# Hash-masked attention and a gated feed-forward block: a hand-written instruction order, transposes on TensorE for the first six pairs, a hash over both heads at once and two-bank accumulators

## The chip, the cores and the metric

The kernel runs on one core of one Trainium2 chip. The core has TensorE (matmuls, PE in the profile), VectorE (DVE), ScalarE (ACT), GpSimd (POOL) and SyncE (SP, which here only starts DMAs). TensorE writes into PSUM, of which the kernel allots eight banks of 512 fp32 numbers per partition. The metric is the device time of one execution in microseconds (us).

## The reference

Inputs are q, k and v of shape (4 batches, 8 heads, 768 tokens, 64), a projection proj (64 x 6), and four weight matrices. Attention is restricted to queries and keys that fall into the same hash bucket; its output is the token matrix x (3072 x 512) of a gated feed-forward block with a gated residual.

```python
q_bits = (np.einsum('bhsd,dk->bhsk', q, proj) > 0).astype(np.int64)
k_bits = (np.einsum('bhsd,dk->bhsk', k, proj) > 0).astype(np.int64)
q_bucket = np.sum(q_bits * 2 ** np.arange(6), axis=-1)   # k_bucket likewise
mask = q_bucket[:, :, :, None] == k_bucket[:, :, None, :]
scores = np.where(mask, scale * np.matmul(q, k.transpose(0, 1, 3, 2)), -1e9)
attn = softmax(scores)                    # with + 1e-09 under the sum
x = (attn @ v).transpose(0, 2, 1, 3).reshape(3072, 512)
...
ffn_out = (gelu(x @ w_gate) * (x @ w_val)) @ w_out
return x + sigmoid(x @ w_res) * ffn_out
```

## The kernel before

Two heads form a pair; there are 16 pairs, four per batch of 768 tokens. The mask needs no comparison: six hash bits of each token, as +0.5 or -0.5, and a constant row are appended to the 64 channels of q and k, scaled so that one differing bit pushes the score far below. So scores of a head contract 71 rows (64 + 6 + 1). A constant 2^-90 times the sum of v keeps a row without any match finite (`L228`).

**Preparation of a pair** (`prep`). q, k and v are loaded by DMA from SP's queue (`load`, L120 and L125). POOL casts q and k to bf16 into the padded tiles `nat` (128 columns per head and token block, L138 and L140). VectorE transposes 32 x 32 blocks of the raw values (`t32`, L168), TensorE multiplies them with `projw` (hash, L175: one matmul per head, half of the channels, and side, 192 columns, four sides next to each other in four column groups of the array). VectorE transposes the sums back (L181) and writes the bits into `nat` with 16 small operations per group of two pairs (L186). Then one DMA transpose per side turns `nat` (12 blocks of 128 x 128, over half padding) into `aug` with channels on partitions (L191). POOL casts v and sums it (L145 to L153).

**Attention** (`scores`, `values`). A head's 768 x 768 score block is cut into banks of 512 columns; a chunk is two banks, nine chunks make a pair. Per chunk: score matmuls into `sp` (L255), one exponential on ScalarE over 1,024 columns (L260), and eight matmuls with the exponentials as weights into the accumulator `av` (L235), which are issued one chunk later. `av` is one bank per head in two rotating buffers. `finish` divides by the sum (L214, L215) into `x_tok` and starts a DMA transpose of the pair's x into `x_sb` (L218).

**Feed-forward** (`gate_val`, `project`). Per batch, `gate_val` runs 12 x 16 matmuls (L276) with a Gelu on ScalarE (L282) and a product on VectorE (L283). `project` is the output side: per token tile, four matmuls of the residual gate (`rps`, L293), a Tanh (L296), twelve matmuls (`fps`, L300) and two VectorE operations (L305, L307), then the store. It is a generator of five pieces per tile; 24 of its 30 pieces are spread over the next batch's chunks, one per chunk, and the last ones (`HELD`) run in the first chunks of the batch after it. `gate_val` of batch b-1 starts in the fourth chunk of batch b (`LEAD = 4`). `rps` and `fps`, the hash sums and the warm-up share the pool `mm_ps`, two rotating buffers of one bank.

**Order.** The Python loop emits the work, and the tile framework's scheduler then orders each engine's instructions by its own estimates. So hash matmuls and single `rps` or `fps` matmuls stand between chunks where the source doesn't put them. DMAs of SP's queue start in that queue's order; a waiting DMA holds those behind it. Fourteen matmuls on zeros (L314) run at the start.

The softmax here doesn't subtract the row's maximum and nothing guards it: scores larger than these inputs give would overflow.

## Time and profile before

| what | us |
|---|---|
| median of 2 runs | 407.17 (406.35 to 407.98) |
| the profiled execution | 406.82 |
| its span, first to last instruction | 404.7 |
| TensorE busy (matmuls) | 366.9, mean granted clock 0.92 |
| ScalarE busy | 206.9 |
| VectorE busy | 170.7 |
| POOL busy | 81.5 |

Groups of instructions that the steps of the prediction use:

```profile
L260 ACT ACTIVATE e<-sp 128x1024 bf16<-128x1024 f32 x144 | 144.4, 1022 | 83.8 <-PE sp L255 82.4
L168 DVE STREAM_TRANSPOSE t<-ld 128x384 f32<-128x384 f32 x64 | 33.8, 557 | 43.8 <-DMA ld<-in_q_dram 21.3
L175 PE MATMUL hs<-t,projw 128*32 128x192 f32 x256 | 27.3, 375 | 17.8 <-DVE t L168 11.7
L186 DVE TENSOR_SCALAR nat<-ht 32x72 bf16<-32x72 f32 x128 | 31.3, 244 | 2.3
```

A line names the source line, the engine, the operation, output<-input with shapes and the count; then busy us in all and mean ns of one; then the idle time of the engine just before these, and what ended it. The page's other parts are the busy share in 40 equal slices, the chain of work that ended last, and the DMA queues: loads of q, k and v land 4.6 to 5.0 us after issue (median), the 32 DMA transposes of q and k 4.9, the 16 of x 3.7, the stores 2.1. HBM traffic is 29.37 MB read and 6.29 MB written.

### The profile page before, as it was taken

The numbers are of one execution on the slowest core, as the hardware profiler recorded it, in microseconds if no ns is written. First come the engines' busy times: TensorE is split into PE (matmuls) and PEld (weight loads), VectorE is DVE, ScalarE is ACT, GpSimd is POOL, SyncE is SP. The second block draws the span as 40 slices with busy tenths as digits, with TensorE's granted clock in tenths as the row PEclk, the third lists the DMA queues.
The fourth block names the chain that finished last, engine by engine and source line by source line (L and its number), as shares of the span: only waits on it lengthen the run. The fifth ranks groups of instructions, "written<-read, shape, count | busy, mean of one in ns | idle before, by whom it ended". The sixth has DMA issues, their size and how long they took to land. (4 is left out here: it accounts for less than half of the span.)

```text
span 404.7 us, 7265 instructions
## 1 busy us (share of the span) xinstructions
PE 366.9 (91%) x2944; PEld 202.2 (50%) x2990; DVE 170.7 (42%) x366; ACT 206.9 (51%) x225; POOL 81.5 (20%) x149
## 2 busy tenths in 40 slices
PE   6386969959999999998999999899999999999995
PEld 2133524425566555554665555556655555565542
DVE  3727123715433324734336537443336232333342
ACT  2036534636332877773335886863357788333210
POOL 7456245344300022241000342310000000000000
PEclk9759555865999999999999999999999999999999
DMA  7999999996910048776000973920008221100012
GB/s 220 223 270 245 159 239 285 201 238 142 238 55 2 28 84 188 137 186 202 2 0 2 185 205 85 185 47 2 0 2 158 76 68 47 45 2 0 16 65 78
DMA packets 86177, 46.61 MB, mean 115 GB/s; under 512 B 64640, under 2 KB 83072, under 8 KB 86144
## 3 DMA queue, kind: packets, MB, share of 16 engines
q1 hardware_dynamic: 79488, 40.91, 44.7%
q0 software_dynamic: 6336, 5.24, 8.7%
q8 instruction: 23, 0.38, 0.4%
q14 instruction: 10, 0.08, 0.1%
q10 hardware_dynamic: 320, 0.01, 0.0%
HBM read 29.37 MB, written 6.29 MB: 88 GB/s over the span
## 5 line engine op out<-in xcount | busy, mean ns | idle before, releaser
L260 ACT ACTIVATE e<-sp 128x1024 bf16<-128x1024 f32 x144 | 144.4, 1022 | 83.8 <-PE sp L255 82.4
L255 PE MATMUL sp<-aug,aug 71*128 71x256 bf16 (+1 forms) x384 | 98.2, 362 | 4.3 <-DMA aug<-nat 4.1
L282 ACT ACTIVATE gt<-sp 128x768 bf16<-128x768 f32 x48 | 38.9, 810 | 83.3 <-PE sp L276 83.3
L283 DVE TENSOR_TENSOR hh<-gt,sp 128x768 bf16<-128x768 bf16 x48 | 45.8, 953 | 81.1 <-PE sp L276 81.1
L235 PEld LDWEIGHTS <-e 128*128 128x128 bf16 x1152 | 54.3, 104 | 43.1 <-ACT e L260 24.0
L276 PE MATMUL sp<-x_sb,wg 128*128 128x512 bf16 (+1 forms) x382 | 72.0, 328 | 2.6 <-DMA x_sb<-x_tok 2.1
L300 PE MATMUL fps<-wo,hh 128*128 128x512 bf16 x265 | 71.4, 379 | 1.7 <-issue 0.5
L276 PE MATMUL sp<-x_sb,wv 128*128 128x512 bf16 (+1 forms) x371 | 70.0, 324 | 1.2 <-DVE hh L283 0.5
L235 PE MATMUL av<-va,e 128*128 128x65 bf16 x1152 | 66.1, 204 | 2.2 <-ACT e L260 1.1
L168 DVE STREAM_TRANSPOSE t<-ld 128x384 f32<-128x384 f32 x64 | 33.8, 557 | 43.8 <-DMA ld<-in_q_dram 21.3
L276 PEld LDWEIGHTS <-wg 128*128 128x128 bf16 x384 | 37.5, 98 | 28.1 <-issue 3.9
L255 PEld LDWEIGHTS <-aug 71*128 71x128 bf16 x384 | 34.8, 105 | 32.4 <-issue 6.5
L276 PEld LDWEIGHTS <-wv 128*128 128x128 bf16 x384 | 37.7, 98 | 25.8 <-issue 1.2
L175 PE MATMUL hs<-t,projw 128*32 128x192 f32 x256 | 27.3, 375 | 17.8 <-DVE t L168 11.7
L300 PEld LDWEIGHTS <-hh 128*128 128x128 bf16 x288 | 24.3, 97 | 24.0 <-issue 5.3
L305 DVE SCALAR_TENSOR_TENSOR o<-th,fps 128x512 f32<-128x512 f32 x24 | 16.4, 683 | 39.4 <-PE fps L300 29.6
L186 DVE TENSOR_SCALAR nat<-ht 32x72 bf16<-32x72 f32 x128 | 31.3, 244 | 2.3
L214 DVE RECIPROCAL rec<-av 128x6 f32<-128x6 f32 x32 | 6.0, 187 | 56.0 <-PE av L235 56.0
L138 POOL TENSOR_SCALAR nat<-ld 128x768 bf16<-128x768 f32 x15 | 12.4, 829 | 73.8 <-DMA aug<-nat 73.8
L296 ACT ACTIVATE th<-rps 128x512 f32<-128x512 f32 x24 | 14.3, 596 | 21.0 <-PE rps L293 17.7
L145 POOL CAST va<-ldv 128x768 bf16<-128x768 f32 x16 | 13.2, 822 | 57.2 <-PE av L235 52.5
L293 PE MATMUL rps<-wr,x_sb 128*128 128x512 bf16 x88 | 24.3, 382 | 0.1
(34 smaller groups left out, 152.9 us busy)
## 6 DMA issues: line engine op xcount, KB each, us to landing
ld<-in_q_dram SPq DMA_DIRECT2D x16, 384.0 KB, 4.7
ld<-in_k_dram SPq DMA_DIRECT2D x16, 384.0 KB, 4.6
ldv<-in_v_dram SPq DMA_DIRECT2D x16, 384.0 KB, 5.0
out_dram<-o SPq DMA_DIRECT2D x24, 256.0 KB, 2.1
wg<-in_moe_w_gate_dram POOLq DMA_DIRECT2D x4, 384.0 KB, 9.6
wv<-in_moe_w_val_dram POOLq DMA_DIRECT2D x4, 384.0 KB, 7.1
wo<-in_moe_w_out_dram POOLq DMA_DIRECT2D x3, 512.0 KB, 10.7
aug<-nat SPq DMA_TRANSPOSE x32, 4.9
```

The source lines that it names most:

```text
L168: nc.vector.transpose(tt.rearrange("p c h n -> p (c h n)"), raw[x][:, h * T:(h + 1) * T].rearrange("p c d -> p (c d)"))
L175: nc.tensor.matmul(hs[32 * j:32 * j + 32, h * T:(h + 1) * T, :], projw[:, dh, :], tt[:, :, dh, :], start=(dh == 0), stop=(dh == 1), tile_p ...
L186: nc.vector.tensor_scalar(nat_of(x)[32 * a:32 * a + 32, :, D:D + NBITS], ht[32 * j:32 * j + 32, :, NBITS * a:NBITS * (a + 1)], 0.0, 0.5, o ...
L235: nc.tensor.matmul(av[p, hi][:, qt, :], e[:, off:off + P], va[:, hi, jt, 0:D + 1], start=False, stop=(jt == T - 1), skip_group_check=True)
L255: nc.tensor.matmul(sp[:, off:off + nq * P], ks[0:KA, hi * T + jt, :], qs[0:KA, hi * T + qt0:hi * T + qt0 + nq, :], start=True, stop=True)
L260: nc.scalar.activation(e, sp, AF.Exp, scale=float(ALPHA))
L276: nc.tensor.matmul(sp[:, c0:c1], w[:, kk, bass.ts(m, P)], xs[:, kk, c0:c1], start=(kk == 0), stop=(kk == KM - 1))
L282: nc.scalar.activation(gt, sp[:, 0:S], AF.Gelu)
L283: nc.vector.tensor_mul(hh[:, m, :], gt, ps[1][:, 0:S])
L293: nc.tensor.matmul(rps, x_sb[b][:, kk, t, :], wr[:, kk, :], start=(kk == 0), stop=(kk == KM - 1))
L300: nc.tensor.matmul(fps, hh[:, m, bass.ts(t, P)], wo[:, m, :], start=(m == 0), stop=(m == KF - 1))
L305: nc.vector.scalar_tensor_tensor(o, th, 1.0, fps, op0=ALU.add, op1=ALU.mult)
```

## The change

- **Order.** `manual_schedule` is switched on: each engine runs its instructions in the order in which the source emits them. The generators are replaced by a list of tasks per chunk (`at(slot, f, ...)`); 144 slots, one per chunk. In a slot stand the scores of the chunk, the slot's tasks, pieces of the projection, and the values of the chunk before.
- **Layout.** A chunk covers one bank of each head instead of two banks of one. `nat` is no longer padded: both heads' 64 channels share 128 columns, so a transpose has six blocks. Its result holds head 0 on partitions 0 to 63 (`aug`, with the mask rows behind them, 71 rows) and head 1 on 64 to 127; POOL copies the latter to a tile of its own (`move_second`), where the mask rows stand on partitions 0 to 6 and zeros up to 63, so that its scores contract 128 rows.
- **Transposes.** For pairs 0 to 5 TensorE transposes q and k (12 matmuls of 128 columns per pair, `transpose_pe`) and VectorE (for pair 0 ScalarE) copies them out of PSUM. The other ten pairs keep the DMA transpose, at half the size. x is transposed on TensorE for batch 0 and for the last pair of each batch, else by DMA; this now happens in the second chunk of the next pair.
- **Hash.** One VectorE block transpose per side covers both heads (768 columns). The matmuls contract 32 rows instead of 128 and have 384 columns; two row groups and four column groups are used. The sums come out with hash bits on partitions, so VectorE writes the bits in two operations per group (`hash_bits`), and small DMAs put them, 7 rows at a time, into `aug` and `second` (`mask_rows`).
- **Accumulators.** `av_ps` and `mm_ps` have one buffer of two banks each instead of two of one bank. `av` holds both heads of a pair; `acc` holds `rps` and `fps` of a row. Hash sums and transposes use the same buffer of `mm_ps`, and whoever takes it first runs the open projection row to its end (`rows_open`). In the last projection both pools alternate.
- **Else.** `LEAD` is 5, loads of the first pairs are issued ahead of everything, weight loads have slots of their own, the warm-up is 8 and 6 matmuls, and the Gelu of the first gate block precedes the last values of the chunk before.

```diff
-    KA = D + NROW
+    ctx.enter_context(tc.manual_schedule(engines=None))
...
-    av_ps = ctx.enter_context(tc.tile_pool(name="av_ps", bufs=2, space=PSUM))
-    mm_ps = ctx.enter_context(tc.tile_pool(name="mm_ps", bufs=2, space=PSUM))
+    av_ps = ctx.enter_context(tc.tile_pool(name="av_ps", bufs=1, space=PSUM))
+    mm_ps = ctx.enter_context(tc.tile_pool(name="mm_ps", bufs=1, space=PSUM))
...
+    def move_second(x, eng):
+        eng.tensor_copy(second[x[0] % NM][x[1]][D:P], aug[x][D:P])
+    def transpose_pe(p):
+        tp = mm_ps.tile([P, 2, 1024], BF16, tag="mm", name="tp")
+        for side in range(2):
+            n = nats.pop((p, side)).rearrange("p t h d -> p t (h d)")
+            for t in range(T):
+                nc.tensor.transpose(tp[:, side, t * P:(t + 1) * P], n[:, t, :], ident)
...
+    def hash_mm(jobs, a0, ps=mm_ps, tag="mm"):
+        while rows_open:
+            mlp_piece()
+        hs = ps.tile([P, 2, 512], FP32, tag=tag, name="hs")
+        for dh in range(2):
+            for j, x in enumerate(jobs):
+                for i in range(2):
+                    a = a0 + i
+                    nc.tensor.matmul(hs[32 * j:32 * j + 32, i, 0:HT * 32],
+                                     projw[32 * a:32 * a + 32, dh, :],
+                                     t32[x][32 * a:32 * a + 32, :, dh, :],
+                                     start=(dh == 0), stop=(dh == 1),
+                                     tile_position=(32 * a, 32 * j))
...
+    def hash_bits(jobs, a0):
...
+        nc.vector.tensor_scalar(dst, hs, 0.0, cst[:n], op0=ALU.is_gt, op1=ALU.add)
+    def mask_rows(jobs, xs, eng=nc.sync):
...
+            for h, dst in ((1, second[x[0] % NM][x[1]][0:NROW]), (0, aug[x][D:D + NROW])):
+                eng.dma_start(dst, bits[jobs[0]][32 * j:32 * j + NROW, h * T:(h + 1) * T])
...
+    def x_transpose(p):
+        b, hp = divmod(p, HP)
+        xt = x_tok[b][:, hp]
+        if b == 0 or hp == HP - 1:
+            while rows_open:
+                mlp_piece()
+            tp = mm_ps.tile([P, T, P], BF16, tag="mm", name="tp")
+            for t in range(T):
+                nc.tensor.transpose(tp[:, t, :], xt[:, t, :], ident)
+            nc.vector.tensor_copy(x_sb[b][:, hp], tp)
...
-            rps = mm_ps.tile([P, DMODEL], FP32, tag="mm", name="rps")
+            acc = ps.tile([P, 2, DMODEL], FP32, tag=tag, name="acc")
+            rps, fps = acc[:, 0, :], acc[:, 1, :]
...
+            rows_open.append(t)
             yield
-            fps = mm_ps.tile([P, DMODEL], FP32, tag="mm", name="fps")
...
+    for g in range(1, NPAIR // 2):
+        s0 = 18 * (g - 1) + (3 if g == 1 else 0)
+        pa, pb = 2 * g, 2 * g + 1
+        jobs = pair_jobs(pa, pb)
+        for i, x in enumerate(jobs):
+            at(s0 + 2 * (i // 2), cast, x, nc.gpsimd)
+            at(s0 + 1 + i, blocks, x)
+        for i, p in enumerate((pa, pb)):
+            s1 = s0 + 2 + 3 * i
+            if g < 3:
+                at(s1, transpose_pe, p)
+                for side in range(2):
+                    at(s1, transposed, (p, side), nc.vector)
+                    at(s1 + 2 + side, move_second, (p, side), nc.gpsimd)
+            else:
+                for side in range(2):
+                    at(s1, transpose_dma, (p, side))
+                    at(s1 + 5 + side, move_second, (p, side), nc.gpsimd)
+        at(s0 + 8, hash_mm, jobs, 0)
+        at(s0 + 8, hash_bits, jobs, 0)
+        at(s0 + 10, hash_mm, jobs, 2)
+        at(s0 + 10, hash_bits, jobs, 2)
+        at(s0 + 11, mask_rows, jobs, jobs[:2])
+        at(s0 + 14, mask_rows, jobs, jobs[2:])
...
+    for s in (20, 22, 28, 30, 36, 37, 38, 39):
+        at(s, load_w)
+    for s in (40, 40, 40, 40):
+        at(s, load_w)
...
+    LEAD = 5
+    for s in range(NSLOT):
+        p, c = divmod(s, NCH)
+        b, slot = divmod(s, NCH * HP)
+        new = scores(p, c)
+        for f in tasks[s]:
+            f()
+        if b >= 1:
+            if slot < LEAD:
+                mlp_piece()
+                mlp_piece()
+            elif mlp and mlp[0][1] < 5 * T - HELD:
+                mlp_piece()
+        flush()
+        pending.append(new)
+        if c == 1 and p >= 1:
+            x_transpose(p - 1)
+        if b >= 1 and slot == LEAD - 1:
+            while mlp:
+                mlp_piece()
+            gate_val(b - 1)
+            mlp.append([project(b - 1), 0])
```

In the built program the new source lines are: L154 warm-up, L188 transposes on TensorE, L195 and L197 the copies out of PSUM, L226 hash, L242 bits, L249 mask rows, L284 and L285 the division, L297 and L298 transpose of x and its copy, L309 and L316 values, L335 scores, L339 exponentials, L354 gate and value matmuls, L375 and L382 the projection's two groups, L387 and L389 its VectorE operations.

## The prediction, made before the changed kernel was run

> **What bounds the kernel now.** I read the page's slices first, then the busy time cut at the stages, then the granted clock in narrow windows, then TensorE's timeline.
>
> ```profile
> span 404.7 us, 7265 instructions
> PE 366.9 (91%) x2944; PEld 202.2 (50%) x2990; DVE 170.7 (42%) x366; ACT 206.9 (51%) x225; POOL 81.5 (20%) x149
> PE   6386969959999999998999999899999999999995
> ...
> PEclk9759555865999999999999999999999999999999
> DMA  7999999996910048776000973920008221100012
> ```
>
> Each digit is 10.1 us. The first ten slices differ from all others: TensorE runs at half clock there, with holes, and the DMA engines are full.
>
> ```profile
> 0.00:21.70 21.70, 9.78 (x48) 4.00 (x48) 11.10 (x32) 2.12 (x2) 12.80 (x28) 0.85 1.02 221
> 21.70:101.10 79.40, 66.64 (x539) 33.04 (x543) 33.73 (x92) 41.45 (x41) 36.37 (x64) 0.63 1.12 222
> ...
> 132.20:182.50 50.30, 48.74 (x516) 27.50 (x522) 22.59 (x54) 39.24 (x42) 12.68 (x24) 1.00 0.59 126
> 182.50:216.30 33.80, 31.83 (x202) 19.16 (x203) 12.56 (x16) 11.44 (x15) 1.95 (x4) 1.00 0.19 60
> ```
>
> Columns: window and length, busy PE, PEld, DVE, ACT, POOL, then clock, DMA share, GB/s. Batch 0's attention (21.7 to 101.1) has 41.5 us of exponentials in 79.4 us; its clock averages 0.63. A later batch's attention with the previous batch's output projection takes 50.3 at clock 1.00, PE busy 48.7. So the first 101 us are bound by transfers and clock, the rest by TensorE's work. In stages: 101.1 before the first feed-forward, 31.1 for it, then attention plus feed-forward 84.1, 84.8 and 78.2, and a tail of 25.4; sum 404.7.
>
> ```profile
> 36.13 10.23 SPq L191 DMA_TRANSPOSE aug<-nat  x2
> 40.11 0.85 PE L175 MATMUL hs<-t,projw 128*32 128x192 f32 x2 [2.85 <-DVE t L168]
> 85.76 0.87 PE L175 MATMUL hs<-t,projw 128*32 128x192 f32 x8 [4.38 <-DMA x_sb<-x_tok]
> ```
>
> The transposes hold SP's queue for 10 us (start, length, then what; in brackets the idle time before), later loads stand behind them, and TensorE idles.
>
> ```profile
> 39.00:40.00 1.00, 0.00 (x0) 0.00 (x0) 0.94 (x5) 0.00 (x0) 0.00 (x0) 0.64 1.30 199
> 55.00:73.00 18.00, 17.85 (x128) 8.41 (x129) 8.18 (x22) 8.18 (x8) 7.35 (x14) 0.50 1.25 254
> 73.00:74.00 1.00, 0.93 (x12) 0.67 (x12) 0.95 (x5) 0.41 (x1) 0.51 (x2) 0.80 1.22 203
> ```
>
> Idle time halves the clock (0.64 in 39:40 puts the fall at 39.3), and 18 us of unbroken attention did not restore it until 73.4.
>
> **Part 1: the start, and batch 0.** Removed: twelve padded DMA transposes of q and k (12 blocks each, median 4.9 us, up to 10 per two) and four of x. First scores: projw lands at 8.2 as before; the hash of pair 0, 16 matmuls, took 1.5, so 9.7; the two bit passes are 768-element VectorE operations, 0.95 each (rows: 552 ns for 384, 953 for 768), the first beside the hash: 11.2; four small mask-row DMAs issue in about 0.45 and land in 2.1 (the output row) to 5.0 (the load row). That is 13.8 to 16.7; I take 14.5, since the loads are nearly through by then. Before: 21.7.
>
> From there 41 chunks run until the first feed-forward (LEAD grows by one). A full-clock chunk costs TensorE 0.435 (scores) + 0.245 (eight av) = 0.68, and ScalarE 1.0 (four exponentials in 3.97). ScalarE bounds: 14.5 + 0.6 + 40 x 1.0 = 55.1. What exceeds the slack of 0.32 per chunk is added:
> - The av accumulator is now one pair of banks, not two rotating ones. Each next pair waits for drain 0.17, reciprocal 0.19, one 768-element multiply 0.95 and gaps, about 1.4 after the last av; one score buffer ahead hides little. 1.3 x 4 boundaries = 5.2.
> - Transposes on TensorE: 12 per pair, between 0.031 each (av steps, 65 columns) and 0.109 (the 256-column step of L276); I take 0.06, 0.7 per pair, 0.4 beyond slack, x 5 = 2.0. The copies out are 2 x 0.95 on VectorE beside it. The x transposes fall into the boundary wait.
> - Hash: 16 matmuls are spaced 0.049 (0.79 for 16) and the weights stay 32 columns wide; moving columns double to 384 (0.32 us a round, estimated from the 326 ns of one with 192). If row groups overlap as the column groups do, a call is 0.8; two short calls 0.6. Beyond slack 0.3 x 2 + 0.5 x 4 + 0.3 behind one x copy = 2.9. Without overlap of row groups a call is 1.28.
> - Cold clock at the first chunks: 1.4. Reason it should then rise: clock changes lie at 39.3, 73.4, 83.6 and 100.7, multiples of 3.41 apart. Weighting each matmul by its rows, the window before 73.4 holds about 76% and 46.1 to 49.5, which stayed cold, 71% (estimates from the timeline). The second head's scores now contract 128 rows, not 71, which makes about 85%.
>
> First feed-forward at 66.6, instead of 101.1: 34.5 gained. SP gets eight mask-row DMAs per group (0.45 to issue each, 3.6), which wait for the bits; the loads behind them are for pairs 9 to 18 chunks later, and that covers them; without it a load's 4.7 would show. VectorE loses 16 bit operations of 0.244 per group (3.9) and gains four copies (3.8); POOL gains four half-height copies per group. Weights: 3.1 MB of gate and value chunks are issued at chunks 36 to 39; at the 383 to 390 GB/s of 101 to 103 us they land in 8 us, the last being needed 23 us into the feed-forward. I cost them at nothing; at 222 GB/s they take 14, still in time.
>
> The Trainium skill, "TensorE: Matmul & The Clock Gate", Part 1, says that one busy window of about 3.4 us restores full clock; the row above (18 us at 0.50) contradicts it for this pattern. By the page the cold start stays near the 1.4 taken; by the row it would be 14 cold chunks, 8 us, and the total 403.
>
> Part 4 of the same page gives about 275 ns for a transpose in a kernel and says that transposes do not count as activity for the clock. No row here shows one; with it the 84 transposes after the start would cost some 16 us more and the total would be about 412.
>
> **Part 2: the later batches.** TensorE's own work in 36 chunks: 24.5 + 8 x 0.17 (L228) + 6 output rows x 16 x 0.2155 = 20.7 + hash 3.2 + x transpose 0.4 = 50.2. New waits, all in TensorE's fixed order: hash and x transposes share the single two-bank accumulator of the output rows, so the open row is first run to its end. Then TensorE waits for drain and L305 (0.17 + 0.68 + 0.05 = 0.9), and the next row waits for the bits (drain 0.2 + 0.95 + 0.05 = 1.2); scores and av queue behind. In chunks 8 and 10 of a batch both: 4.2; a third hash 0.9; the last x transpose 0.9; one av boundary 0.4. Sum 6.4. Forced pieces also use up the projection by chunk 23, so some 12.5 chunks run at ScalarE's 1.0 instead of 0.68: 4.0. That is 60.6, plus 31.2 for the feed-forward = 91.8 (twice), where before had 84.1 and 84.8. The last batch has 31 chunks to itself: 45.0 work, 7.3 waits (2.2 of them at the end, in place of the 2.8 us DMA transpose of x), 3.9 thin chunks, 31.2 = 87.4, before 78.2. Half-size q/k transposes remain in SP's queue; they are issued 13 to 16 chunks before use, which hides them. If that failed, 3 to 5 us each.
>
> **Sum.** 66.6 + 31.2 + 91.8 + 91.8 + 87.4 + 25.4 = 394.2. The profiled execution lasted 406.82 with a span of 404.7, so 2.1 lies around; the median (407.17) is 0.35 higher. Forecast 396.5: 34.5 gained in front, 24 given back later.
>
> **Rivals.**
> - *The waits cost more* (402 to 413): POOL carries half-copies, value sums (2.97 a pair) and casts in one order; pair 2's casts may come 3 us late for chunk 5. Hash calls at 1.28 add 0.48 x 14 = 6.7. Together 406. For it: hand order cannot step around a late operand. Against: VectorE's bit runs, which cost 0.7 at 170 before, are gone.
> - *The waits hide* (376 to 387): front 61, half of the 24 returned; 379. For it: ScalarE's floor is 55; against it, in-order TensorE.
> - *Half clock through batch 0* (slower): after the hash TensorE waits some 3 us for mask rows, as the 2.85 us hole did before the fall at 39.3. Cold chunks cost 1.28 (two in 47.35 to 49.91): 41 x 1.28 + 3 + transposes 10.2 + hash 8.8 + 1 = 75.5, first feed-forward at 90, total 420. It decides from about 33 cold chunks of 41 (0.57 each; 18.6 us more than the forecast passes the 2% line); at 18 the gain is gone.
> - That the change doesn't do what it says is excluded by the built program's order: transposes and forced rows stand where the diff puts them.
>
> **How the numbers follow.** Forecast case (387 to 402) 0.40, of which 0.07 above 399; waits cost more 0.24; waits hide 0.14; half clock, or hash tiles that do not overlap at all, 0.22. Over 2% faster (below 399.0): 0.33 + 0.14 = 0.47. Within 2%: 0.31. Slower: 0.22. Two per cent is about what a measurement of this kernel tells from none. The range 380 to 420 leaves out half of each outer case, 0.18.
>
> **What would show it.** First scores near 14.5; exponentials about 1.0 apart until 66.6 with 1.3 us holes at four pair boundaries; clock 1.00 from about 20; L226 calls of 0.8; 0.9 and 1.2 us holes before L226 and L375; attention stages of about 60. A clock of 0.50 past 40 us, transposes above 0.1 each, or a first feed-forward later than 77 would make it wrong.

## The result, and the profile after

The changed kernel takes **431.97 us** (median of two runs, 430.43 to 433.5), the kernel before 407.17. The ratio is 1.061, 95% interval 1.042 to 1.080: about 6% slower, where 396.5 was forecast. The profiled execution of the changed kernel is the one of 430.43 us, with a span of 428.6.

The page of the changed kernel, its head and the slices:

```profile
span 428.6 us, 7961 instructions
PE 367.1 (86%) x3301; PEld 202.5 (47%) x3360; DVE 154.1 (36%) x201; ACT 208.6 (49%) x227; POOL 108.1 (25%) x187
PE   7688788999789887999779988999869976999884
...
PEclk9999999999799999999999999999998998999999
DMA  7343989980030590900012490700020100000011
```

A digit is now 10.7 us. The first ten digits are no longer what differs from the rest: the clock is up and the DMA engines have gaps. What is new are the sevens and eights in TensorE's row behind the first feed-forward, where there was a row of nines. TensorE is busy as long as before (367.1 against 366.9) at a higher mean clock (0.98 against 0.92), so it has more work, and behind the front more holes.

The same busy times cut at the stages (window and length, busy PE, PEld, DVE, ACT, POOL, then clock, DMA share, GB/s): to the first scores, batch 0's attention, the three later attention stages, the tail.

```profile
0.00:15.65 15.65, 9.62 (x58) 4.13 (x59) 7.41 (x12) 3.62 (x4) 9.49 (x25) 1.00 0.55 182
15.65:71.97 56.32, 45.49 (x673) 26.68 (x684) 28.00 (x40) 39.55 (x41) 44.77 (x73) 1.00 0.75 172
103.71:172.62 68.91, 57.62 (x604) 30.04 (x614) 24.87 (x34) 39.38 (x43) 14.71 (x26) 0.95 0.35 89
204.36:270.52 66.16, 55.06 (x605) 29.07 (x614) 24.88 (x34) 39.39 (x43) 14.70 (x26) 1.00 0.34 93
302.26:366.60 64.34, 51.90 (x496) 27.02 (x504) 14.94 (x22) 36.58 (x39) 0.00 (x0) 0.95 0.11 32
397.96:428.60 30.64, 21.62 (x95) 9.14 (x94) 9.23 (x13) 3.58 (x6) 0.00 (x0) 0.97 0.14 52
```

Batch 0 went nearly as planned: 56 us at clock 1.00 (forecast 52) in place of 79 at 0.63. The later attention stages are the surprise: 11 us of each of the first two pass without a busy TensorE, where the kernel before had 1.6 to 1.8. Even the tail, which has nothing but the last output projection, grew from 25.5 to 30.6.

The table of waits names the holes. It is TensorE's, in total, times, and the longest:

```profile
PE av L316 <- ACT e L339: 12.3, 28, 0.7
PE acc L382 <- ACT th L378: 8.4, 12, 0.8
PE acc L375 <- DVE bits L242: 7.0, 6, 1.2
PE hs L226 <- DVE o L387: 6.7, 8, 0.9
PE av L309 <- DVE x_tok L285: 4.9, 7, 1.1
PE sp L335 <- DMA aug<-bits: 4.5, 2, 3.5
PE tp L297 <- DVE o L387: 2.9, 3, 1.3
```

Lines 3, 4, 5 and 7 are the waits that the prediction priced, at about the prices it gave. Line 1 is TensorE waiting for exponentials: 4.7 us of it lie in batch 0, where ScalarE sets the pace, and 2.4 to 2.7 in each later stage, where the prediction had 4.0 for thin chunks. Line 6 belongs to batch 0 (the mask rows of its first pairs). Line 2 is one that the prediction did not have: the first feed-forward matmul of an output row (L382) waits for ScalarE's Tanh (L378). Six of the twelve stand in the tail, one per row, as the timeline shows (start, length, engine, what; in brackets the idle time before):

```profile
398.86 0.60 ACT L378 ACTIVATE th<-acc 128x512 f32<-128x512 f32 x1 [1.35 <-PE acc L375]
399.51 2.75 PE L382 MATMUL acc<-wo,hh 128*128 128x512 bf16 x12 [0.69 <-ACT th L378]
402.09 1.03 PE L375 MATMUL acc<-wr,x_sb 128*128 128x512 bf16 x4
403.16 0.60 ACT L378 ACTIVATE th<-acc 128x512 f32<-128x512 f32 x1 [3.70 <-PE acc L375]
403.81 2.75 PE L382 MATMUL acc<-wo,hh 128*128 128x512 bf16 x12 [0.69 <-ACT th L378]
```

A row takes 403.81 - 399.51 = 4.30 us, of which 0.69 is the wait. The Tanh reads the residual half of the accumulator, the matmul writes the other half. In the kernel before these were two tiles; now both are halves of one two-bank tile, and the write waits for the read of the whole tile.

### The profile page after: what moved, and what is told of

The parts are those of the page before. It is cut to its first block, busy times and chain, and to the rows that moved or that the text cites. A ratio compares the mean times of both kernels' runs of the same rounds, so it can differ in the third digit from the quotient of the medians.

```text
span 428.6 us, 7961 instructions
## 1 busy us (share of the span) xinstructions
PE 367.1 (86%) x3301; PEld 202.5 (47%) x3360; DVE 154.1 (36%) x201; ACT 208.6 (49%) x227; POOL 108.1 (25%) x187
## 5 line engine op out<-in xcount | busy, mean ns | idle before, releaser
L339 ACT ACTIVATE e<-sp 128x1024 bf16<-128x1024 f32 x144 | 143.7, 1022 | 66.9 <-PE sp L335 58.5
L382 PE MATMUL acc<-wo,hh 128*128 128x512 bf16 x275 | 72.6, 388 | 9.5 <-ACT th L378 8.4
L316 PEld LDWEIGHTS <-e 128*128 128x128 bf16 x1152 | 51.8, 98 | 54.7 <-ACT e L339 34.9
L316 PE MATMUL av<-va,e 128*128 128x65 bf16 x1152 | 62.3, 195 | 13.4 <-ACT e L339 12.3
L354 PE MATMUL sp<-x_sb,wg 128*128 128x256 bf16 (+1 forms) x378 | 69.9, 325 | 0.3
L354 PE MATMUL sp<-x_sb,wv 128*128 128x512 bf16 (+1 forms) x374 | 69.7, 324 | 0.5
L335 PE MATMUL sp<-aug,aug 71*128 71x512 bf16 x192 | 55.6, 330 | 4.5 <-DMA aug<-bits 4.5
L382 PEld LDWEIGHTS <-hh 128*128 128x128 bf16 x288 | 28.4, 99 | 44.0 <-issue 17.8
L354 PEld LDWEIGHTS <-wg 128*128 128x128 bf16 x384 | 37.3, 98 | 25.0 <-issue 0.5
L354 PEld LDWEIGHTS <-wv 128*128 128x128 bf16 x384 | 37.4, 98 | 24.4
L335 PE MATMUL sp<-second,second 128*128 128x256 bf16 (+1 forms) x171 | 47.5, 323 | 0.0
L387 DVE SCALAR_TENSOR_TENSOR o<-th,acc 128x512 f32<-128x512 f32 x24 | 16.4, 684 | 79.4 <-PE acc L382 60.8
L179 POOL COPY second<-aug 64x768 bf16<-64x768 bf16 x32 | 25.8, 826 | 66.3 <-DMA aug<-nat 57.9
L378 ACT ACTIVATE th<-acc 128x512 f32<-128x512 f32 x24 | 14.3, 596 | 57.7 <-PE acc L375 57.4
L226 PE MATMUL hs<-t,projw 32*32 32x384 f32 x512 | 27.7, 509 | 7.9 <-DVE o L387 6.7
L375 PE MATMUL acc<-wr,x_sb 128*128 128x512 bf16 x88 | 25.4, 393 | 9.5 <-DVE bits L242 7.0
L284 DVE RECIPROCAL rec<-av 128x12 f32<-128x12 f32 x16 | 3.7, 232 | 75.6 <-PE av L316 75.6
L201 DVE STREAM_TRANSPOSE t<-ld 128x768 f32<-128x768 f32 x32 | 29.3, 952 | 2.2 <-DMA ld<-in_q_dram 2.2
L242 DVE TENSOR_SCALAR bits<-hs,cst 128x768 bf16<-128x768 f32 (+1 forms) x18 | 18.2, 1015 | 23.5 <-PE hs L226 23.5
## 6 DMA issues: line engine op xcount, KB each, us to landing
wo<-in_moe_w_out_dram POOLq DMA_DIRECT2D x3, 512.0 KB, 17.8
```

Of the source, the lines that this page charges most:

```text
L179: eng.tensor_copy(second[x[0] % NM][x[1]][D:P], aug[x][D:P])
L201: nc.vector.transpose(tt.rearrange("p c h n -> p (c h n)"), raw[x].rearrange("p c d -> p (c d)"))
L226: nc.tensor.matmul(hs[32 * j:32 * j + 32, i, 0:HT * 32], projw[32 * a:32 * a + 32, dh, :], t32[x][32 * a:32 * a + 32, :, dh, :], start=(dh ...
L316: nc.tensor.matmul(o[:, qt, :], e[:, off:off + P], va[:, hi, jt, 0:D + 1], start=False, stop=(jt == T - 1), skip_group_check=True)
L335: nc.tensor.matmul(sp[:, off:off + nq * P], ks[0:n, jt, :], qs[0:n, qt0:qt0 + nq, :], start=True, stop=True)
L339: nc.scalar.activation(e, sp, AF.Exp, scale=float(ALPHA))
```

## The experiments

All times of a stage below run from the end of the last gate or value matmul (the feed-forward's L354) to the start of the next feed-forward's first. By this cut the first feed-forward of the kernel before starts at 98.2; the prediction, which put the matmuls that its scheduler mixed with attention to the attention, had 101.1. "Total" is the median of a kernel's runs (one run each for the hash on half its columns and for 6, two to ten for the others); "span" and the stages are those of the one profiled execution.

| run | total | span | first gate | attention, batch 1 / 2 / 3 | without half clock | tail |
|---|---|---|---|---|---|---|
| before | 407.17 | 404.7 | 98.2 | 50.2 / 51.4 / 45.4 | | 25.5 |
| changed | 431.97 | 428.6 | 72.0 | 68.9 / 66.2 / 64.3 | 65.5 / 66.2 / 60.9 | 30.6 |
| 1 split accumulator | 414.14 | 410.8 | 75.5 | 62.3 / 62.3 / 58.5 | 62.3 / 62.3 / 56.8 | 25.7 |
| 2 no piece beside the hash | 423.42 | 420.7 | 74.6 | 63.9 / 63.9 / 61.1 | 63.9 / 63.9 / 59.4 | 30.7 |
| 3 hash on half its columns | 427.17 | 425.3 | 70.7 | 66.2 / 66.5 / 64.6 | 64.5 / 64.8 / 59.5 | 30.7 |
| 3 hash in one call, four banks | 418.78 | 415.5 | 72.6 | 63.5 / 63.4 / 58.7 | 63.5 / 63.4 / 57.0 | 30.7 |
| 4 scheduler's order | 414.57 | 412.9 | 90.5 | 59.5 / 56.9 / 47.3 | 59.5 / 56.9 / 47.3 | 25.4 |
| 5 pairs 2 to 5 transposed by DMA | 434.12 | 431.7 | 75.7 | 67.9 / 67.6 / 62.9 | 66.2 / 65.9 / 61.2 | 30.7 |
| 5 av one chunk later | 433.57 | 429.9 | 73.1 | 68.2 / 67.3 / 64.4 | 64.8 / 65.6 / 59.3 | 30.7 |
| 5 fillers before the first scores | 430.88 | 429.3 | 72.5 | 69.0 / 66.2 / 64.4 | 65.6 / 66.2 / 61.0 | 30.7 |
| 5 finer projection pieces | 429.35 | 426.3 | 71.9 | 67.5 / 67.4 / 62.2 | 65.8 / 65.7 / 60.5 | 30.7 |
| 6 split, and half the hash columns | 403.35 | 401.6 | 70.4 | 61.8 / 59.9 / 57.3 | 60.1 / 59.9 / 55.6 | 25.6 |
| 7 all in one | 377.23 | 373.8 | 71.5 | 52.5 / 52.5 / 45.2 | 52.5 / 52.5 / 45.2 | 25.6 |
| 7 all in one, second version | 376.21 | 373.0 | 70.7 | 52.3 / 52.3 / 45.6 | 52.3 / 52.3 / 45.6 | 25.6 |

The column "without half clock" is an estimate. In the windows of one microsecond the clock is 0.50 for stretches of 3.4 us (or two on end) in many of these stages, not always in the same ones from kernel to kernel; 1.7 us is taken off for each stretch, half of its length, as for work that TensorE bounds. It makes the stages comparable; the totals hold all of it. In the changed kernel these stretches are 113.0 to 119.8 (two), 321.2 to 324.6 and 362.1 to 365.5.

The feed-forwards are 31.4 to 32.1 us in all of these but the kernel before and the scheduler's last one, which mix attention or projection into them. The kernel before ran at a median of 407.2 beside the changed kernel, and at 409.0, 409.0, 410.9 and 411.4 beside the other groups of runs. So the totals of two groups can differ by up to some 4 us for reasons that have nothing to do with the edit; smaller effects are read from the stages.

### 1. The accumulator in two tiles

```diff
-            acc = ps.tile([P, 2, DMODEL], FP32, tag=tag, name="acc")
-            rps, fps = acc[:, 0, :], acc[:, 1, :]
+            rps = ps0.tile([P, DMODEL], FP32, tag=tag0, name="rps")
+            fps = ps1.tile([P, DMODEL], FP32, tag=tag1, name="fps")
...
-    for _ in project(B - 1, ((mm_ps, "mm"), (av_ps, "av"))):
+    for _ in project(B - 1, ((mm_ps, "r", mm_ps, "f"), (sc_ps, "sp", sc_ps, "sp"))):
```

> Only the accumulator is taken apart: the residual half (rps) and the feed-forward half (fps) of a row get a one-bank tile each, the hash and the transposes use the same two one-bank tiles, and the order of instructions stays. Theory A (the two-bank tile makes the first feed-forward matmul of a row, L382, wait for the Tanh that reads the other bank; 8.4 us in 12 waits in the changed kernel, plus some 0.7 per row where the wait is partly hidden): the waits of that matmul for ScalarE vanish, a row of the tail takes 3.6 instead of 4.3 us, the tail 26 to 27 instead of 30.8, and the whole comes out 8 to 11 us lower, at 421 to 424. The hash bits become two operations of 0.55 (384 elements) instead of one of 1.02, so the wait of L375 for the bits falls from 1.17 to about 0.75, another 2.5. Rival B (the rows are bound by the rate of the matmuls and the wait only moves to the next instruction): tail still 30 to 31, total 429 to 433.

Measured: 414.14 us, ratio to before 1.012 (1.007 to 1.017); the span is 17.8 lower than the changed kernel's. The tail is 25.7. Theory A holds in kind and was too small. The same place in the tail, split kernel (L381 the residual, L384 the Tanh, L388 the feed-forward half):

```profile
391.90 1.03 PE L381 MATMUL rps<-wr,x_sb 128*128 128x512 bf16 x4
...
392.76 2.75 PE L388 MATMUL fps<-wo,hh 128*128 128x512 bf16 x12
...
392.96 0.60 ACT L384 ACTIVATE th<-rps 128x512 f32<-128x512 f32 x1 [2.85 <-PE rps L381]
```

The feed-forward half now starts before its Tanh does, and TensorE's lines have no idle time in brackets. A row takes 3.45 (392.76 after 389.31).

The later stages give 6.6, 3.9 and 5.8 us back, with the tail 21.2. By the estimate without half clock it is 3.2, 3.9 and 4.1, with the tail 16.1; the other 5.1 are three stretches fewer. Of the 16.1 the tables of waits behind the first feed-forward account for some 14: 8.4 for Tanh, 2.5 for the bits (4.5 instead of 7.0; they come in two operations of 0.61, each of which frees a bank), 1.7 for L375's waits for the row before and for the x copy (1.0 and 0.7, now none), 1.2 for exponentials (6.4 instead of 7.6). The rest was not followed. The 6.7 us of waits for o in front of the hash are gone from the split kernel's table, but not from its time: only the first of the hash's two banks is free early, so the wait now stands inside the hash's row, which is 2.44 long where the changed kernel has 0.86 of idle time and 1.52.

```profile
112.83 2.44 PE L230 MATMUL hs<-t,projw 32*32 32x384 f32 x32
```

How the clock fell beside such holes is seen behind the first hash of batch 1 in the changed kernel (columns as in the stages above):

```profile
110.00:111.00 1.00, 0.24 (x2) 0.00 (x0) 0.64 (x1) 0.01 (x1) 0.00 (x0) 1.00 0.00 0
111.00:112.00 1.00, 0.90 (x24) 0.49 (x32) 0.74 (x2) 0.00 (x0) 0.00 (x0) 1.00 0.00 0
112.00:113.00 1.00, 0.62 (x16) 0.10 (x1) 0.27 (x1) 0.00 (x0) 0.00 (x0) 0.98 0.34 129
113.00:114.00 1.00, 0.20 (x1) 0.10 (x1) 0.75 (x1) 0.00 (x0) 0.00 (x0) 0.50 0.36 133
...
118.00:119.00 1.00, 1.00 (x11) 0.69 (x10) 0.25 (x2) 0.08 (x1) 0.00 (x0) 0.50 0.00 0
```

The wait for o leaves 110 to 111 nearly empty, the wait for the bits 112.6 to 113.8. The clock falls at 113.0 and is at 0.50 until 119.8, from 115 on through work that has no hole in it. But the second hash of batch 2, with the same two holes, has no fall:

```profile
220.00:221.00 1.00, 0.59 (x16) 0.34 (x24) 0.97 (x2) 0.00 (x0) 0.00 (x0) 1.00 0.00 0
221.00:222.00 1.00, 0.93 (x24) 0.25 (x9) 0.08 (x1) 0.00 (x0) 0.00 (x0) 1.00 0.11 31
222.00:223.00 1.00, 0.00 (x0) 0.00 (x0) 0.96 (x1) 0.00 (x0) 0.00 (x0) 1.00 0.65 236
```

So such holes can be followed by a fall, and need not be; what decides it no run here shows. The split kernel's front is 3.5 us later than the changed kernel's: its profiled execution has 14.4 to 21.2 and 45.1 to 48.5 at half clock, where the changed kernel's has 1.00 throughout batch 0.

The Trainium skill, "Perfetto Trace Analysis", section "Matmuls", asks that independent matmul groups rotate through PSUM banks, so that one group's evacuation overlaps the next group's matmuls. Here the two groups were in two banks already; sharing a tile was enough to lose the overlap, and two tiles brought it back.

### 2. No projection piece in the hash's chunk

```diff
-            elif mlp and mlp[0][1] < 5 * T - HELD:
+            elif slot not in (8, 10) and mlp and mlp[0][1] < 5 * T - HELD:
```

> No piece of the output projection is emitted in the two chunks of a batch that hold a hash call (chunks 8 and 10 of batches 1 to 3), so that values and scores, not the first matmul of the next row, stand behind the hash. Theory A (the 1.17 us waits of L375 for the bits are real idle time, and the holes around the hash also drop the clock): the six waits go (7.0 us), and the stretches at half clock (112.9 to 119.8 and 321.4 to 324.6 in the changed kernel, some 4 us of lost time) shrink or go; total 421 to 426. Rival B (the idle time only moves: the piece is run later in a chunk that already has TensorE work, or the hash waits longer for the row before it): total within 2 us of 432.

Measured: 423.42 us, ratio 1.036 (1.029 to 1.043); span 7.9 lower, stages 5.0, 2.3 and 3.2 lower (1.6, 2.3 and 1.5 without half clock). Theory A. The wait of L375 for the bits falls from 7.0 to

```profile
PE acc L375 <- DVE bits L242: 1.2, 3, 0.4
```

and of the four half-clock stretches in the later stages one is left (354.3 to 357.7). What stays are the waits in front of the hash and the Tanh's.

### 3. The length of a hash call: columns or instructions

```diff
-                    nc.tensor.matmul(hs[32 * j:32 * j + 32, i, 0:HT * 32],
+                    nc.tensor.matmul(hs[32 * j:32 * j + 32, i, 0:T * 32],
                                      projw[32 * a:32 * a + 32, dh, :],
-                                     t32[x][32 * a:32 * a + 32, :, dh, :],
+                                     t32[x][32 * a:32 * a + 32, 0:T, dh, :],
```

> The hash matmuls stream 192 columns instead of 384 (the second head's hash is left out and the first head's bits are written for both; number of matmuls unchanged). Theory A (a call is bound by the columns that pass through one tile position: four rounds of 0.32 and 0.15 around): a long call falls from 1.46 to about 0.8, the total by about 9 us for 14 calls, less where it was hidden in batch 0. Rival B (a call is bound by the number of matmuls, 32 records at 0.046): the call stays at 1.4 to 1.5.

The second run of this group makes both calls of a hash one, over four banks:

```diff
+        pair = [ps.tile([P, 2, 512], FP32, tag=tag, name="hs"),
+                sc_ps.tile([P, 2, 512], FP32, tag="sp", name="hs2")]
...
-                for i in range(2):
-                    a = a0 + i
-                    nc.tensor.matmul(hs[32 * j:32 * j + 32, i, 0:HT * 32],
+                for a in range(4):
+                    nc.tensor.matmul(pair[a // 2][32 * j:32 * j + 32, a % 2, 0:HT * 32],
```

> Both calls of a group are made one: all four row groups of the hash write four banks (the accumulator's two and one score buffer), 32 matmuls in one call, in the chunk of the first call; the bits are still two operations of 768. Theory A (columns bound it and four row groups run beside each other as two do): one call of 1.5 to 1.8 in place of two of 1.46, and one forced row, one wait for o (0.85) and one wait for the bits (1.17) less in each of the three late batches: 3 x (1.3 + 2.0) and about 2 in front, total 418 to 424. Rival B (issue of 64 records binds, or row groups beyond two queue): the call takes 2.9, only the waits are saved, total 424 to 428; the score buffer that it takes holds the next scores back by up to 1 us each time, which could eat the rest.

One call in the changed kernel, a short call (two jobs instead of four) in the same kernel:

```profile
31.93 1.52 PE L226 MATMUL hs<-t,projw 32*32 32x384 f32 x32 [0.21 <-DVE x_sb L298]
...
18.31 1.49 PE L226 MATMUL hs<-t,projw 32*32 32x384 f32 x16
```

with half the columns:

```profile
118.08 0.88 PE L226 MATMUL hs<-t,projw 32*32 32x192 f32 x32 [0.85 <-DVE o L388]
```

and with four row groups in one call:

```profile
111.73 1.92 PE L228 MATMUL hs<-t,projw 32*32 32x384 f32 x64 [0.86 <-DVE o L388]
```

One fp32 matmul is two records here (x32 for 16 matmuls). Half the records with the same columns take the same time (1.49), the same records with half the columns take 0.88, twice the records in four row groups 1.92. So the columns that pass through one tile position set most of the time, and the tiles run beside each other; where the 0.4 of sixteen tiles over eight come from was not followed. A call is 1.5 and a group of two calls 3.0. The kernel before had two calls of 0.86 by the same measure, one of them this:

```profile
155.86 0.86 PE L175 MATMUL hs<-t,projw 128*32 128x192 f32 x16
```

In time, halving the columns gave 3.3 of span, where 14 long calls shorter by 0.64 are 9. Without half clock the late stages fall by 1.0, 1.4 and 1.4, where four, four and two shorter calls are 2.6, 2.6 and 1.3. The wait for the bits grew (7.8 instead of 7.0), and what is missing beyond that was not followed; in the span there is also a fifth half-clock stretch. One call of four banks gave 418.78 (1.026, 1.017 to 1.035), span 13.1 lower, stages 2.0, 2.8 and 3.9 lower without half clock: theory A, since it also takes one forced row and its two waits out of each batch. The call is longer than the 1.5 to 1.8 expected, and the next scores do wait for the score buffer lent to the hash, 4.6 us in five waits, as rival B feared.

### 4. The order: by hand or by the scheduler

```diff
-    ctx.enter_context(tc.manual_schedule(engines=None))
```

> Only the line that fixes the order by hand is taken out; the scheduler orders each engine's instructions as it did in the kernel before. Theory A (the waits come from the shared two-bank accumulator and from the hash's length, not from the order): the tail stays near 30.8 (nothing else stands in it to be moved), the later attention stages stay above 60, total 424 to 436. Rival B (the fixed order itself costs the time, since nothing can step past a late operand; a scheduler would put scores and values ahead of the waiting hash and L375): the 17 us of waits around hash and x transposes go, total 412 to 418.

Measured: 414.57 us (1.014, 1.010 to 1.018). Rival B, against my theory, the tail above all: 25.4. The scheduler's tail, same tiles, same accumulator:

```profile
388.62 5.34 PE L381 MATMUL acc<-wo,hh 128*128 128x512 bf16 x24 [0.47 <-ACT th L377]
393.80 2.02 PE L374 MATMUL acc<-wr,x_sb 128*128 128x512 bf16 x8
```

It takes the residual halves of two rows first (x8) and then their feed-forward halves (x24), so the second row's matmuls cover the first row's Tanh. The table of waits has 0.5 us for Tanh in all, where the changed kernel has 8.4. The shared tile makes a wait possible; the fixed order exposes it. In front the sides are exchanged: the first feed-forward is at 90.5 instead of 72.0, with the clock halved from 17.0 to 34.1, 54.6 to 61.4 and 81.9 to 88.7. So the hand order gains 18.5 us in front and loses 34 behind it.

### 5. What the front's gain is made of

Pairs 2 to 5 back on SP's queue (the condition `g < 3` becomes `g < 1`):

> Pairs 2 to 5 are transposed by SP's queue again, in the half-size form that the changed kernel uses for the later pairs, and not on TensorE; pairs 0 and 1 stay on TensorE. Theory A (the front's gain comes from keeping transposes out of SP's full queue): the first feed-forward moves from 72 to between 80 and 90, as the loads stand behind the transposes again, and the total rises by 8 to 18. Rival B (the gain comes from the smaller, unpadded transposes and the new start; TensorE's transposes only cost it 0.8 each pair): first feed-forward at 68 to 74, total within 3 us of the changed kernel.

First feed-forward 75.7, total 434.12: the total is rival B's, the front stands between the two ranges, nearer to B's. Two half-size transposes hold the queue 2.6 to 4.4 us in this front, two padded ones held it 10.2 before. The 3.7 us by which the front is later come with 10 us at half clock (17.2 to 20.6, 44.5 to 51.4) that the changed kernel's lacks. So TensorE's transposes of these pairs are worth at most 3.7 us, and how much of that is the clock this run doesn't show.

The av boundary:

```diff
-        flush()
+        if c != 1 or p == 0:
+            flush()
         pending.append(new)
-        if c == 1 and p >= 1:
+        if c == 2 and p >= 1:
```

> The weighted sums (av) of a pair's first chunk are emitted one chunk later, together with those of its second, and the x transpose one chunk later too, so that scores and a projection piece stand between the last av of a pair and the first write of the next pair to the single av accumulator. Theory A (the boundary wait, 4.9 us in 7 waits, is idle time of TensorE on the path in batch 0): it goes, first feed-forward 3 to 4 earlier, total 4 to 6 lower, 426 to 428. Rival B (ScalarE's exponentials set the pace of batch 0, and the wait is only slack): the wait goes, first feed-forward within 1 us of 72, total within 2 of 432.

The wait falls from 4.9 to 0.2, the first feed-forward stays (73.1), and the total too (433.57, 1.060, 1.056 to 1.064). That is rival B's outcome, but not its proof: L375 waits 2.4 more for o, and batch 0 has two stretches at half clock (15.5 to 18.9, 66.7 to 70.1) that the changed kernel's lacks, which could hide up to 3.4.

Fillers ahead of the first scores (`warm_up(6)` becomes `warm_up(16)`):

> Sixteen instead of six filler matmuls stand between the first hash and the first scores, so that TensorE works through its wait for the mask rows (3.5 us, at 14.5 to 20 the clock is at 0.50 in all runs so far). Theory A (the cold first chunks are due to that idle time): clock 1.00 from the first scores on, first feed-forward 1.5 to 3 earlier, total about 2 lower. Rival B (the clock falls from what lies before, or the front is paced by something else): cold stretch as before or moved, first feed-forward within 1 of 72.

First scores at 16.2, first feed-forward at 72.5, total 430.88: rival B. The expectation had one thing wrong: the clock is low behind the first scores in the variants run before it, but not in the changed kernel's profiled execution, so this run had no cold start to remove. It shows that a front without one is no faster than 72.

What paces the front, none of these three shows, but ScalarE's timeline of the changed kernel does. Between the first and the last of the 41 exponentials ScalarE is idle for 15.1 us, in 13 places, each behind something that kept TensorE from the next scores. Four of them:

```profile
31.82 1.02 ACT L339 ACTIVATE e<-sp 128x1024 bf16<-128x1024 f32 x1 [1.16 <-PE sp L335]
34.34 1.94 ACT L339 ACTIVATE e<-sp 128x1024 bf16<-128x1024 f32 x2 [1.49 <-PE hs L226]
37.26 3.97 ACT L339 ACTIVATE e<-sp 128x1024 bf16<-128x1024 f32 x4 [0.98 <-PE sp L335]
54.94 1.94 ACT L339 ACTIVATE e<-sp 128x1024 bf16<-128x1024 f32 x2 [1.21 <-PE sp L335]
```

The first stands behind a pair boundary, the other three behind a hash call of 1.5. Six holes behind hash calls make 8.8 (the longest, 2.31, has a boundary in it too), three boundaries 3.7, transposes 1.3, a wait for mask rows 1.3. The prediction had 2.9 for the hash, 5.2 for four boundaries, 2.0 for transposes and 1.4 for a cold clock, 11.5 in all. With half the hash columns (experiment 3) the three holes shown behind hash calls are each 0.64 shorter, as much as the call:

```profile
34.77 1.94 ACT L340 ACTIVATE e<-sp 128x1024 bf16<-128x1024 f32 x2 [0.85 <-PE sp L336]
37.05 3.97 ACT L340 ACTIVATE e<-sp 128x1024 bf16<-128x1024 f32 x4 [0.34 <-PE sp L336]
54.21 1.94 ACT L340 ACTIVATE e<-sp 128x1024 bf16<-128x1024 f32 x2 [0.57 <-PE sp L336]
```

So the length of a hash call is on the path in the front as well. Moving the boundary by a chunk, as the second of these runs did, put it in front of the next burst: at 34.79 ScalarE has one hole of 2.47 there, in place of 1.16 and 1.49.

Finer pieces of the projection (two matmuls, 12 pieces held):

> A projection row is cut into pieces of two feed-forward matmuls instead of three (seven pieces a row, 12 held back), so that they reach through more of a batch's chunks; all else as in the changed kernel. Theory A (the thin chunks at the end of a batch, bound by the exponentials, cost the 4.0 per batch of the prediction): attention stages 2 to 4 lower, total 422 to 427. Rival B (forced rows use the pieces up all the same, and the waits set the stages): stages within 1 us, total 430 to 433.

The total is 2.6 lower (429.35). The stages move by -1.4, +1.2 and -2.1, and by +0.3, -0.5 and -0.4 without half clock, with one half-clock stretch now in each stage: rival B, with a total just below its range. In this order finer pieces bring next to nothing.

### 6. Do the two causes make up the miss?

Experiment 1 with half the hash columns on top:

> The split accumulator together with the hash on half its columns (the second head's hash is left out and the first head's bits are written for both heads). Theory A (the two terms missing from, or too small in, the forecast of the later batches are the wait for Tanh and the length of a hash call, and nothing else of size): attention stages 60, 60 and 56 as forecast (60.6, 60.6, 56.2), tail 25.7, total 403 to 408 with a first feed-forward at 70 to 75. Rival B (something further is missing, such as the clock falling in the now larger holes beside a short hash, as it did in five stretches with the half hash alone): stages stay at 62 and 58, total 410 or more.

Measured, in a single run: 403.35 us, stages 61.8, 59.9 and 57.3, tail 25.6. Theory A. The first and last stage each hold one stretch at half clock (110.6 to 114.0, 339.3 to 342.7); without it the three are 60.1, 59.9 and 55.6, beside 60.6, 60.6 and 56.2 forecast. So with the two causes out, the stages are at their forecast. The parts agree less well than the sum: in batch 2 TensorE is busy 53.8 us, where the forecast had 50.2 of work, and idle 6.1, where it had 6.4 of waits and 4.0 of thin chunks. That nothing else was mis-sized is therefore not shown; two errors partly cancel.

### 7. A kernel that beats both

Split accumulator; one hash call over four banks, at a row's end in mid-batch or just ahead of the feed-forward; x transposes into the residual half's bank, without closing the row; pieces of two matmuls; av one chunk later.

```diff
-            elif mlp and mlp[0][1] < 5 * T - HELD:
+            elif mlp and mlp[0][1] < 7 * T - HELD:
                 mlp_piece()
-        flush()
+        if s + 1 in late:
+            while rows_open:
+                mlp_piece()
+        if c != 1 or p == 0:
+            flush()
+        if s in late:
+            hash_mm(late[s])
+            hash_bits(late[s])
...
+            hash_mm(gate_hash[b])
+            hash_bits(gate_hash[b])
             gate_val(b - 1)
```

> All in one: one-bank accumulators for the two halves of a row; a hash of all four row groups in one call over four banks, put at row ends or just ahead of a feed-forward, so that no half-open row has to be run to its end in front of it; projection pieces of two matmuls in place of three, so that they last through all chunks of a batch; x transposes into the residual half's bank, without closing the row; the av lag of one chunk at a pair's start. Theory A (the later stages are TensorE's work plus the waits that the single runs show): attention stages 53 to 55, 53 to 55 and 48 to 50, tail 25.7, first feed-forward at 66 to 70, total 376 to 386. Rival B (removed waits uncover others: the exponentials, the score buffer lent to the hash, VectorE): stages of 58 to 60, total 395 to 403.

Measured: **377.23 us**, ratio to before 0.923 (0.920 to 0.925). Theory A's total; the front did not get the gain it hoped for (71.5, with one half-clock stretch from 15.5 to 18.9), the stages did better. Page and waits of this kernel:

```profile
PE   7588788999999999999999999999999998999994
...
PEclk9899999999999999999999999999999999999999
```

```profile
PE av L324 <- ACT e L347: 4.5, 11, 0.7
PE sp L343 <- DMA aug<-bits: 4.2, 1, 4.2
PE sp L343 <- ACT e L347: 1.9, 4, 0.9
PE av L317 <- DVE x_tok L295: 1.4, 4, 0.5
```

Behind the first feed-forward TensorE's row is nearly all nines again and the clock never falls; Tanh, bits and o are out of the list of long waits. A second version (transposes of one side per chunk, fillers, a lead of four):

> The combined kernel with three small things more: sixteen filler matmuls ahead of the first scores, the transposes of pairs 2 to 5 cut into one side per chunk (six instead of twelve at a time), and a lead of four instead of five chunks with the second hash of a batch one chunk earlier. Theory A (in batch 0 each burst on TensorE longer than the slack of 0.32 under an exponential delays the chain of exponentials by the rest): first feed-forward 67 to 69 instead of 71.5, total 371 to 375. Rival B (the front is paced by VectorE's and GpSimd's copies behind the transposes): first feed-forward 71 to 72, total 376 to 378.

376.21 us (0.918, 0.914 to 0.922), first feed-forward 70.7: nearer to rival B, total and front. The two versions can't be told apart.

## Why the prediction was wrong

The span is 34.4 over the sum of 394.2: the front 5.4 (72.0 for 66.6), four feed-forwards 1.7 (31.6 for 31.2 each), the later attention stages 8.3, 5.6 and 8.1, the tail 5.2.

**The step that failed** is the list of new waits in part 2, and with it the tail, carried over at its old 25.4. The diff made one tile of two accumulators. I used that for hash and x transposes, which need the open row closed, and did not ask who else touches the two halves: the Tanh reads one while L382 wants the other. The waits for it are 8.4 us, 4.1 of them in the tail. The split run shows them to be on the path: its tail is 4.9 shorter, its three stages 11.2, of which 4.3 are Tanh and the rest what the split does besides (bits, the wait for the row before, exponentials, some not followed), and 5.1 more are clock.

**The hash was mis-sized**: "16 matmuls are spaced 0.049 (0.79 for 16)" read 16 records as 16 matmuls. They were eight, and a call priced at 0.8 is 1.5. The line just behind it had the right handle, 0.32 a round, and "Without overlap of row groups a call is 1.28" had the right size for the wrong reason: the row groups do overlap, each call uses only two of four, and a matmul is two rounds. In batches 1 and 2 that is four calls x 0.7 = 2.8 more, in batch 3 two calls; beside the split run, half the columns give 2.2, 2.4 and 1.2 (without half clock). In the front it is the largest part of what went wrong: ScalarE's holes behind hash calls are 8.8, for 2.9 forecast, while first scores came 1.2 late and a wait for mask rows of 1.3 was not in the sum. In batch 2, which has no half clock, the hash's 2.8 and Tanh's 1.5 make 4.3 of the 5.6 missed.

**The clock behind the front** was taken at 1.00. In the later stages it was at half for 13.6 us, worth some 7 by the estimate above. The three falls lie in or just behind a wait: of L375 for the bits at 113.0 and 321.2, of L382 for Tanh at 362.1; with the Tanh wait or the bits wait removed, one stretch of the four was left. That the holes are the reason is argued from this and not proven: the same holes in batch 2 have no fall, and the variants that keep both waits in full have three to six stretches.

**Right**: the waits of L226 (0.85) and L375 (1.18) against 0.9 and 1.2; first scores at 15.65 against 14.5; transposes at 0.83 for twelve, 0.07 each against 0.06; SP's queue out of the way; the gain in front, 29 of 34.5; the price of a pair boundary, 1.2 to 1.4 where it stands alone. The clock of 1.00 through batch 0 came true in the profiled execution, partly by luck: of the eleven other kernels in hand order, nine have a stretch at half clock behind their first scores. The thin chunks show as 2.4 us of waits for exponentials per batch instead of 4.0, and finer pieces did not bring them back.

**Rivals.** *The waits cost more* is the one that happened, beyond its 413: not through POOL, which it named, but through the hash, which it named at 1.28 a call, and through ScalarE's Tanh, which it did not name. *Half clock through batch 0* is out: the clock is 1.00 there, and low for 3 to 10 us behind the first scores in those variants in hand order that have it low at all, not for 33 chunks. *The waits hide* is out by the table of waits. On the rule of the Trainium skill, "TensorE: Matmul & The Clock Gate", Part 1: in the changed kernel the stretch from 113.0 ends after 6.8 us, of which the second 3.4 are fully busy, as the page says; in the scheduler's version of the same kernel the clock stayed at 0.50 from 17 to 34, with TensorE's row busy throughout from 20 on. What tells the two apart no run here shows. Part 4's 275 ns per transpose is not this kernel's price: one record lasts 0.22, but twelve follow each other within 0.83.

## What to carry to other kernels

When a change merges two buffers into one tile, list every reader and writer of both halves, not only the operations that the change brings: a reader on another engine becomes a wait at each turn of the loop, and where the order is fixed nothing steps around it. Price a stage that the diff seems not to touch only after checking that none of its tiles changed. Count how many records an instruction leaves before dividing a time by their number.

A fixed order has to be written around the waits: the same parts in hand order, with the hash at row ends and both halves split, went from 6% slower to 8% faster. What the scheduler would make of those parts was not run, so that the hand order itself pays is not shown.

## What the runs showed of the hardware

- 32x32 tiles of fp32 matmuls in all four row groups and four column groups run beside each other: 64 records of 384 columns in 1.92 us, where 32 records in two row groups take 1.52.
- Holes of about 1 us can be followed by half clock, and need not be: TensorE was 24, 90 and 62% busy in the three microseconds before the fall at 113.0, and 59, 93 and 0% from 220 to 223, with no fall. In the later stages of the hand-ordered kernels a stretch lasts 3.4 us, or 6.8 as two on end. The half hash has five stretches of 3.4 there and the lagged av six, where the changed kernel has four, so by the estimate above part of what they saved went to the clock.
